# Gate logits of six token tiles summed on VectorE instead of multiplied on TensorE, and new distances between the operands in SBUF

## The chip, the cores and the metric

The kernel runs on one core of one Trainium2 chip. The metric is the device time of one execution in microseconds (us). A core has TensorE (PE, with its weight loads shown apart as PEld), VectorE (DVE), ScalarE (ACT), GpSimd (POOL) and SyncE (SP, which issues most DMAs). Each engine takes its instructions in the order written, and waits for the others through semaphores.

## The reference

Windowed attention makes 1152 token rows of 512 columns. A first mixture of four experts with given weights follows, then a second mixture of eight experts, where a gate sends each token to one expert:

```python
x = attention(q, k, v)                        # (1152, 512), window of 64
for e in range(4):                            # first mixture: every token, every expert
    out += p[:, e:e+1] * (maximum(x @ w1[e], 0) @ w2[e])
x = out
logits = x @ w_gate + modality_bias[modality_id]     # w_gate is (512, 8)
e_idx = argmax(logits, axis=1)
gate_w = softmax(logits)[arange(N), e_idx]
for e in range(8):                            # second mixture: a token's own expert alone
    h = maximum(x[e_idx == e] @ m2w1[e], 0)
    out[e_idx == e] = gate_w * (h @ m2w2[e])
```

The change touches `x @ w_gate`, for tokens 0 to 767, and where the tensors of all layers lie.

## The kernel before

**Tiles and stages.** The 1152 tokens are nine tiles of 128. A product in full precision is three products of rounded parts: tokens x are held as `xh` + `xl`, hidden rows as `hh` + `hl`, weights as `wh` + `wl`. Expert 0 runs interleaved with the attention. Experts 1, 2 and 3 each run over three groups g of 384 tokens (`moe1_group`): a **first layer** of eight blocks f (`mm1_at`, 12 matmuls of 384 columns each, weights stationary, tokens moving, line L343), then a **second layer** of three token tiles j in four parts each (`mm2_part`, 6 matmuls of 512 columns per part, hidden rows stationary, weights moving, L368). The second mixture follows in slots of 256 or 352 tokens with the same two layers.

**What follows a block.** After block f ACT writes `hh` (L352), then DVE writes `hl` (L353); that frees the block's PSUM bank. There are three such banks in turn, shared by both layers: block f=3 uses the bank of f=0, the second layer's tile j=0 that of f=5. After tile j DVE adds the result to `acc` (L379). Part p of tile j=0 reads `hl` of blocks 2p and 2p+1.

**Hooks.** After each block or part a hook may issue other work; the order is written by hand. In expert 3 the gate's logits are made one group later than their tokens: in group 1 for tiles 0 to 2, in group 2 for tiles 3 to 5. `gate_T` turns a token tile with four PE transposes (L751) and splits it in three bf16 parts (two ACT, two DVE instructions: L754 to L757); `gate_L` does twelve bf16 matmuls of 24 columns (L767); `gate_V`, after f=4, makes softmax and choice on DVE in a chain of small instructions, each waiting for the one before. `select_P` (after f=6 of group 1, one small matmul `psC`, L813) and `phase1` (after f=6 of group 2, two matmuls `psR`, L828 and L829) follow it. Tiles 6 to 8 are gated later.

**Where tensors lie.** In bytes of a partition, modulo 512, the built program has: the identity `ident` 128; `xh`, `xl`, `hh`, `hl`, `acc` and all `wh`, `wl` 384. Their column slices and blocks are multiples of 512 bytes apart, but the token tiles of `acc` are 2080 bytes apart, as are the seven buffers `xr` of gathered tokens.

Of the kernel before, what the change touches and what calls it, by code (L numbers as in the profile page):

```python
# [5 lines left out]
F32 = mybir.dt.float32  # L6
# [3 lines left out]
ACTF = mybir.ActivationFunctionType  # L10
ALU = mybir.AluOpType
# [4 lines left out]
def build(tc, q, k, v, probs, w1, w2, mid, wg, mbias, m2w1, m2w2, out):  # L16
    nc = tc.nc
    B, H, S, D = q.shape
    E, DM, FF = w1.shape
    NT = B * S  # L20
    NTILE = NT // 128
    HP = H // 2
    KD = DM // 128
    KF = FF // 128
    G0, G1 = 128, 256
    GT = 384
    NG = NT // GT
    ctx = ExitStack()
    with ctx:
        const = ctx.enter_context(tc.tile_pool(name="const", bufs=1))  # L30
# [11 lines left out]
        ident = const.tile([128, 128], F32, name="ident")  # L42
        mk = const.tile([128, 3, 128], F32, name="mk")
        prob = const.tile([128, NTILE, E], F32, name="prob")
        psumw = const.tile([128, 24], F32, name="psumw")[:, 0:NTILE].rearrange("p (t o) -> p t o", o=1)
        xh = big.tile([128, HP, NT], F32R, name="xh")
        xl = big.tile([128, HP, NT], F32R, name="xl")
        hh = big.tile([128, KF, GT], F32R, name="hh")
        hl = big.tile([128, KF, GT], F32R, name="hl")
        acc = big.tile([128, NTILE, 520], F32, name="acc")  # L50

        ident4 = big.tile([128, 56], F32, name="ident4")[:, 0:32]

        with tc.manual_schedule():

# [335 lines left out]
            def moe1_group(e, c0, n, hook):  # L391

                for f in range(KF):
                    mm1_at(f, c0, n)
                    hook("1", f, 0)
                mm2_group(e, c0, n, hook)
# [58 lines left out]
            def L(fn, *a):  # L455
                return lambda: fn(*a)
# [191 lines left out]
            for i in range(4):  # L648
# [36 lines left out]
            OHC = m2.tile([128, NTILE + 1, E2], BF16, name="OHC")  # L685

            nc.sync.dma_start(out=wgf, in_=wg.rearrange("(c p) e -> p c e", p=128))
            nc.sync.dma_start(out=mb.rearrange("p m e -> p (m e)"),
                              in_=mbias.rearrange("m e -> (m e)").partition_broadcast(128))
            nc.sync.dma_start(out=midi, in_=mid.bitcast(I32).rearrange("(t p w) -> p t w", p=128, w=2))  # L690
# [38 lines left out]
            def vv(out, a, b, op):  # L729
                nc.vector.tensor_tensor(out=out, in0=a, in1=b, op=op)  # L730
# [7 lines left out]
            def red(out, a, op=ALU.add):  # L738
                nc.vector.tensor_reduce(out=out, in_=a, axis=AX.X, op=op)
# [20 lines left out]
            def gate_L(t):  # L760
# [4 lines left out]
                for c in range(KD):  # L765
                    for i in range(3):
                        nc.tensor.matmul(out=psL[g][:, j], lhsT=x[i][:, c, :], rhs=wgb[:, c],  # L767
                                         start=(c == 0 and i == 0), stop=(c == KD - 1 and i == 2))

            def gate_V(g):  # L770
                sl = slice(3 * g, 3 * g + 3)
                lg = m2.tile([128, 3, E2], F32, tag="lg", name="lg", bufs=2)
                ex = m2.tile([128, 3, E2], F32, tag="ex", name="ex", bufs=2)
                mx = m2.tile([128, 3, 1], F32, tag="mx", name="mx", bufs=2)
                red(lg, psL.pop(g).rearrange("p j i e -> p j e i"))
                vv(lg, lg, biasm[:, sl, :], ALU.add)
                red(mx, lg, ALU.max)
                vv(lg, lg, mx.to_broadcast([128, 3, E2]), ALU.subtract)
                nc.scalar.activation(out=ex, in_=lg, func=ACTF.Exp)

                vs(lg, lg, 0.0, ALU.is_ge)
                vv(lg, lg, rev.to_broadcast([128, 3, E2]), ALU.mult)
                red(mx, lg, ALU.max)
                vv(OH[:, sl, :], lg, mx.to_broadcast([128, 3, E2]), ALU.is_equal)
                nc.vector.tensor_copy(out=OHb[:, sl, :], in_=OH[:, sl, :])
                for t in range(3 * g, 3 * g + 3):
                    vv(OHC[:, t + 1, :], OHC[:, t, :], OHb[:, t, :], ALU.add)
                gt = acc[:, sl, DM:DM + 1]
                red(gt, ex)
                vs(gt, gt, 1e-9, ALU.add)  # L790
                nc.vector.reciprocal(out=gt, in_=gt)
                nc.sync.dma_start(out=x2d[GT * g:GT * (g + 1), :].rearrange("(t p) d -> p t d", p=128),
                                  in_=acc[:, sl, :])
# [252 lines left out]
            def std(g):  # L1046
                def hook(kind, idx, part):
                    if g == 0 and kind == "1" and idx % 2 == 1:
                        split_next()
                    if g == NG - 1 and kind == "2" and idx < 2 and part in (0, 2):  # L1050
                        split_next()
                return hook
# [15 lines left out]

            for e in range(1, E - 1):
                for g in range(NG):  # L1070
                    moe1_group(e, GT * g, GT, std(g))

            def gating(g0):
                t = {}
                for f in range(3):
                    t.setdefault(("1", f, 0), []).append(L(gate_T, 3 * g0 + f))
                    t.setdefault(("1", f + 2, 0), []).append(L(gate_L, 3 * g0 + f))
                t["1", 4, 0].append(L(gate_V, g0))
                return t

            t1 = gating(0)
            t1["1", 6, 0] = [select_P, pump]
            t2 = gating(1)
            t2["1", 6, 0] = [phase1]
            t2["2", 0, 2] = [L(ids_mm, 1, 6)] + [L(gather, 1, a, 2 * GT) for a in range(A1)]
            t2["2", 1, 0] = [between]
# [2 lines left out]
            t2["2", 1, 1] = [L(gate_T, 6)]  # L1089
            t2["2", 2, 0].append(L(gate_L, 6))  # L1090
            t2["2", 2, 2] = [L(gate_T, 7)]
            moe1_group(E - 1, 0, GT, std(0))
            moe1_group(E - 1, GT, GT, at_hook(t1, std(1)))
            moe1_group(E - 1, 2 * GT, GT, at_hook(t2, std(2)))

# [185 lines left out]
```

## Time and profile before

| | |
|---|---|
| three runs | 595.76, 595.93, 595.97 us, median 595.93 |
| the profiled execution | 595.89 us, of which its span in the trace 594.1 us |
| outside the span | 1.79 us |
| PE busy | 585.4 us (99%) |
| DVE busy | 248.6 us (42%) |
| ACT busy | 192.1 us (32%) |
| POOL busy | 83.4 us (14%) |

Matmuls overlap in the pipeline and their ends are modelled, so 99% does not say that PE is at its peak; the distance from one matmul's start to the next one's tells more. Start times of the timeline are us from the span's start.

### The profile page before, as it was taken

The page shows a single profiled execution, that of the slowest core. Times are in us where ns is not written, and L with a number is a line of the kernel's source. Part 1 is how long each engine was busy: PE and PEld are TensorE (multiplying, and loading weights), DVE is VectorE, ACT ScalarE, POOL GpSimd, SP SyncE. Part 2 cuts the span into 40 slices and gives each one's busy share as a digit, 9 for nine tenths or more (in the row PEclk, how much of TensorE's full clock was granted, in tenths as well). Part 3 has the DMA queues.
Part 4 walks back from the last instruction along what each step waited for, and adds up shares of the span by engine and source line. Part 5 has one row for each costly group of instructions (what it writes and reads, how often), then busy time and mean ns, then how long its engine had stood idle before and what let it go on. Part 6 is the DMA issues. An engine that isn't in the chain of part 4 may idle for free. (4 is left out here: it accounts for less than half of the span.)

```text
span 594.1 us, 9420 instructions
## 1 busy us (share of the span) xinstructions
PE 585.4 (99%) x3818; PEld 517.0 (87%) x3818; DVE 248.6 (42%) x534; ACT 192.1 (32%) x373; POOL 83.4 (14%) x129
## 2 busy tenths in 40 slices
PE   8999999999999999999999999999999999999996
PEld 7798797979898989899898989899898989897964
DVE  4954545363462212524121243335168597233410
ACT  5853434352340101313020222222043455233421
POOL 3851212022000000000000000000002105323221
PEclk9999999999999999999999999999999999999999
DMA  8996460000521000224000040002306277316530
GB/s 212 201 254 99 89 196 1 2 2 1 143 76 68 0 1 0 75 67 135 9 0 1 1 142 1 0 1 69 127 2 203 79 269 210 133 54 207 189 90 31
DMA packets 55919, 51.11 MB, mean 86 GB/s; under 512 B 41151, under 2 KB 41151, under 8 KB 55872
## 3 DMA queue, kind: packets, MB, share of 16 engines
q1 hardware_dynamic: 53664, 45.05, 27.7%
q0 software_dynamic: 1680, 5.29, 2.6%
q8 instruction: 31, 0.51, 0.4%
q10 hardware_dynamic: 528, 0.13, 0.1%
q14 instruction: 16, 0.13, 0.1%
HBM read 45.71 MB, written 4.95 MB: 85 GB/s over the span
## 5 line engine op out<-in xcount | busy, mean ns | idle before, releaser
L343 PE MATMUL ps<-xh,wh 128*128 128x384 f32 (+2 forms) x544 | 173.5, 319 | 0.0
L343 PE MATMUL ps<-xh,wl 128*128 128x384 f32 (+2 forms) x544 | 171.7, 316 | 0.0
L343 PE MATMUL ps<-xl,wh 128*128 128x384 f32 (+2 forms) x544 | 171.5, 315 | 0.0
L368 PE MATMUL ps<-wh,hh 128*128 128x512 f32 (+1 forms) x368 | 147.2, 400 | 0.3 <-DVE hl L353 0.3
L368 PE MATMUL ps<-wh,hl 128*128 128x512 f32 (+1 forms) x368 | 144.0, 391 | 0.0
L368 PE MATMUL ps<-wl,hh 128*128 128x512 f32 (+1 forms) x368 | 143.8, 391 | 0.0
L352 ACT ACTIVATE hh<-ps 128x384 fp32r<-128x384 f32 (+2 forms) x112 | 52.0, 464 | 260.4 <-PE ps L343 255.8
L353 DVE SCALAR_TENSOR_TENSOR hl<-ps,hh 128x384 fp32r<-128x384 f32 (+2 forms) x112 | 58.2, 522 | 118.6 <-ACT hh L352 118.6
L343 PEld LDWEIGHTS ps<-xh,wh 128*128 128x128 f32 x544 | 103.0, 189 | 0.9 <-issue 0.3
L343 PEld LDWEIGHTS ps<-xl,wh 128*128 128x128 f32 x544 | 103.0, 189 | 0.5
L343 PEld LDWEIGHTS ps<-xh,wl 128*128 128x128 f32 x544 | 102.9, 189 | 0.0
L368 PEld LDWEIGHTS ps<-wh,hh 128*128 128x128 f32 (+1 forms) x368 | 68.8, 187 | 16.7 <-issue 2.2
L368 PEld LDWEIGHTS ps<-wh,hl 128*128 128x128 f32 (+1 forms) x368 | 68.7, 187 | 15.3
L368 PEld LDWEIGHTS ps<-wl,hh 128*128 128x128 f32 (+1 forms) x368 | 68.8, 187 | 13.3
L379 DVE SCALAR_TENSOR_TENSOR acc<-ps,prob,acc 128x512 f32<-128x512 f32 x27 | 20.3, 750 | 94.9 <-PE ps L368 94.9
L1019 POOL DMA_INDIRECT xr<-x2d,idg x11 | 12.5, 1137 | 317.5 <-DVE ids L730 314.9
L171 DVE TENSOR_TENSOR wl<-raw,wh 128x1024 fp32r<-128x1024 f32 x42 | 52.0, 1253 | 8.8 <-ACT wh L167 8.8
L167 ACT ACTIVATE wh<-raw 128x1024 fp32r<-128x1024 f32 x48 | 49.1, 1052 | 0.0
L277 ACT ACTIVATE sm<-sm,st 128x128 f32<-128x128 f32 x72 | 23.2, 391 | 5.4 <-DVE st L266 5.4
L294 POOL TENSOR_TENSOR sm<-sm,rs 128x512 f32<-128x512 f32 (+1 forms) x20 | 19.5, 976 | 26.3 <-DVE rs L287 24.3
L257 DVE SCALAR_TENSOR_TENSOR sm<-psS,mk 128x256 f32<-128x256 f32 (+1 forms) x40 | 14.0, 391 | 19.0 <-PE psS L245 17.7
L1042 POOL DMA_INDIRECT out_dram<-y,ids x11 | 11.3, 1024 | 58.5 <-ACT y L1040 37.2
(189 smaller groups left out, 413.1 us busy)
## 6 DMA issues: line engine op xcount, KB each, us to landing
raw<-in_moe_w_dram SPq DMA_DIRECT2D x60, 512.0 KB, 4.0
x2d<-acc SPq DMA_DIRECT2D x3, 780.0 KB, 3.8
va<-in_v_dram SPq DMA_DIRECT2D x8, 256.0 KB, 5.1
vb<-in_v_dram SPq DMA_DIRECT2D x16, 128.0 KB, 4.5
acc<-in_moe_w_dram SPq DMA_DIRECT2D x4, 512.0 KB, 8.6
acc<-in_q_dram SPq DMA_DIRECT2D x6, 128.0 KB, 4.3
qu<-in_q_dram SPq DMA_DIRECT2D x3, 256.0 KB, 4.0
ku<-in_k_dram SPq DMA_DIRECT2D x3, 256.0 KB, 4.8
```

The source lines that it names most:

```text
L167: nc.scalar.activation(out=hi, in_=x, func=ACTF.Copy)
L171: eng.tensor_tensor(out=lo[:, o], in0=x[:, o], in1=hi[:, o].bitcast(F32), op=ALU.subtract)
L257: nc.vector.scalar_tensor_tensor(out=p[:, h], in0=ps[:, h, 0:128 * nj].rearrange("p (j c) -> p j c", j=nj), scalar=0.125, in1=m, op0=ALU.m ...
L277: nc.scalar.activation(out=p[:, h, j], in_=p[:, h, j], func=ACTF.Exp, bias=st[:, o:o + 1])
L294: nc.gpsimd.tensor_tensor(out=p, in0=p, in1=rs.rearrange("p (h j) o -> p h j o", h=2).to_broadcast([128, 2, nj, 128]), op=ALU.mult)
L343: nc.tensor.matmul(out=ps[:, 0:n], lhsT=a[kk][:, fs], rhs=b_[:, kk, gs], start=(kk == 0 and term == 0) if first is None else (first and te ...
L352: nc.scalar.activation(out=hi, in_=ps[:, 0:n], func=ACTF.Relu)
L353: nc.vector.scalar_tensor_tensor(out=lo, in0=ps[:, 0:n], scalar=0.0, in1=hi.bitcast(F32), op0=ALU.max, op1=ALU.subtract)
L368: nc.tensor.matmul(out=ps[0:m], lhsT=a[:, f, ts_], rhs=b_[c][:, o:o + 512], start=(f == 0 and i == 0), stop=(f == KF - 1 and i == 2))
L379: nc.vector.scalar_tensor_tensor(out=o, in0=ps, scalar=prob[:, t, e:e + 1], in1=o, op0=ALU.mult, op1=ALU.add)
L1019: nc.gpsimd.indirect_dma_start(out=x, out_offset=None, in_=x2d[0:last, :], in_offset=bass.IndirectOffsetOnAxis(ap=idg[i][:, a:a + 1], axis=0))
L1042: nc.gpsimd.indirect_dma_start(out=out, out_offset=bass.IndirectOffsetOnAxis(ap=ap, axis=0), in_=y[0:m], in_offset=None, bounds_check=NT - ...
```

## The change

Six tiles no longer pass through `gate_T` and `gate_L`. `gate_D(t, e_)` takes one tile and one of the eight experts: a DVE instruction multiplies the tile's 512 columns by that expert's gate weights and sums them along the row into one logit per token. 48 of them are issued, two per hook, 24 for each three tiles: 16 during tiles j=1 and j=2 of one group's second layer, 8 after blocks f=0 to 3 of the next group. All 48 write the same scratch tile `gjunk`. For this the gate's weights must stand in each partition: once, after f=4 of group 1 of expert 1, `turn_wg` turns them with one PE transpose, stores them to DRAM with four DMAs and loads eight rows with eight DMAs that repeat a row in all 128 partitions. The eight rows lie in buffers that later hold gathered tokens and outputs.

Pads and one tensor's place change too. Modulo 512 the built program now has `xh`, `xl` at 480, `hh`, `hl`, `acc`, `wh`, `wl` at 256, `ident` still at 128. So tokens and weights of the first layer, which stood at distance 0, stand at distance 224; hidden rows and weights of the second layer stay at distance 0.

```diff
-        psumw = const.tile([128, 24], F32, name="psumw")[:, 0:NTILE].rearrange("p (t o) -> p t o", o=1)
+        psumw = const.tile([128, 48], F32, name="psumw")[:, 0:NTILE].rearrange("p (t o) -> p t o", o=1)
         xh = big.tile([128, HP, NT], F32R, name="xh")
         xl = big.tile([128, HP, NT], F32R, name="xl")
+        ident4 = big.tile([128, 72], F32, name="ident4")[:, 0:32]
         hh = big.tile([128, KF, GT], F32R, name="hh")
         hl = big.tile([128, KF, GT], F32R, name="hl")
-        acc = big.tile([128, NTILE, 520], F32, name="acc")
-        ident4 = big.tile([128, 56], F32, name="ident4")[:, 0:32]
+        acc = big.tile([128, NTILE * 520 + 56], F32, name="acc")[:, 0:NTILE * 520].rearrange("p (t d) -> p t d", d=520)
...
+            def turn_wg():
+                ps = pa.tile([KD * E2, 128], F32, tag="T", name="psWG")
+                nc.tensor.transpose(out=ps, in_=wgr.rearrange("p c e -> p (c e)"), identity=ident)
+                nc.scalar.activation(out=wgt, in_=ps, func=ACTF.Copy)
+                for c in range(KD):
+                    nc.sync.dma_start(out=wgd[:, 128 * c:128 * (c + 1)], in_=wgt[E2 * c:E2 * (c + 1), :])
+                for e_ in range(E2):
+                    nc.sync.dma_start(out=wge[e_][:, 0:DM], in_=wgd[e_, :].partition_broadcast(128))
...
+            def gate_D(t, e_):
+                nc.vector.scalar_tensor_tensor(out=gjunk, in0=acc[:, t, 0:DM], scalar=1.0, in1=wge[e_][:, 0:DM],
+                                               op0=ALU.mult, op1=ALU.mult, accum_out=lgd[:, t, e_:e_ + 1])
...
             def gate_V(g):
...
-                red(lg, psL.pop(g).rearrange("p j i e -> p j e i"))
-                vv(lg, lg, biasm[:, sl, :], ALU.add)
+                if g < 2:
+                    vv(lg, lgd[:, sl, :], biasm[:, sl, :], ALU.add)
+                else:
+                    red(lg, psL.pop(g).rearrange("p j i e -> p j e i"))
+                    vv(lg, lg, biasm[:, sl, :], ALU.add)
...
             def gating(g0):
-                t = {}
-                for f in range(3):
-                    t.setdefault(("1", f, 0), []).append(L(gate_T, 3 * g0 + f))
-                    t.setdefault(("1", f + 2, 0), []).append(L(gate_L, 3 * g0 + f))
-                t["1", 4, 0].append(L(gate_V, g0))
-                return t
+                before, t = {}, {}
+                for n in range(8):
+                    before["2", 1 + n // 4, n % 4] = [L(gate_D, 3 * g0 + n // 4, 2 * (n % 4) + i) for i in range(2)]
+                for n in range(4):
+                    t["1", n, 0] = [L(gate_D, 3 * g0 + 2, 2 * n + i) for i in range(2)]
+                t["1", 4, 0] = [L(gate_V, g0)]
+                return before, t
```

On DVE, before the change, the end of expert 3's group 0 and the first blocks of group 1 stand so (`ps` and a number is a PSUM bank of a block or tile):

```order
L379 SCALAR_TENSOR_TENSOR acc<-ps_3572,prob,acc 128x512
L379 SCALAR_TENSOR_TENSOR acc<-ps_3598,prob,acc 128x512
L379 SCALAR_TENSOR_TENSOR acc<-ps_3624,prob,acc 128x512
L353 SCALAR_TENSOR_TENSOR hl<-ps_3650,hh 128x384
L755 TENSOR_TENSOR xg<-psGT,xg_3670 128x512
L757 TENSOR_TENSOR xg_3672<-xg,xg_3671 128x512
L353 SCALAR_TENSOR_TENSOR hl<-ps_3678,hh 128x384
L755 TENSOR_TENSOR xg<-psGT,xg_3698 128x512
L757 TENSOR_TENSOR xg_3700<-xg,xg_3699 128x512
```

And with the change (L791 is `gate_D`; x6 is six in a row):

```order
L379 SCALAR_TENSOR_TENSOR acc<-ps_3601,prob,acc 128x512
L791 SCALAR_TENSOR_TENSOR gjunk,lgd<-acc,wge 128x512 x6
L379 SCALAR_TENSOR_TENSOR acc<-ps_3627,prob,acc 128x512
L791 SCALAR_TENSOR_TENSOR gjunk,lgd<-acc,wge 128x512 x8
L379 SCALAR_TENSOR_TENSOR acc<-ps_3661,prob,acc 128x512
L791 SCALAR_TENSOR_TENSOR gjunk,lgd<-acc,wge 128x512 x2
L353 SCALAR_TENSOR_TENSOR hl<-ps_3695,hh 128x384
L791 SCALAR_TENSOR_TENSOR gjunk,lgd<-acc,wge 128x512 x2
L353 SCALAR_TENSOR_TENSOR hl<-ps_3712,hh 128x384
L791 SCALAR_TENSOR_TENSOR gjunk,lgd<-acc,wge 128x512 x2
```

The second layer, where DVE had one instruction per tile, now holds sixteen `gate_D`, and two stand between any two `hl` of the next first layer's first blocks, in the place of L755 and L757.

On PE, before the change, the seam between blocks f=1 and f=2 of expert 3's group 1 reads (`psGT` is the bank of the turned tile):

```order
L343 MATMUL ps_3678<-xl,wh_3397 128x384
L343 MATMUL ps_3678<-xh,wl_3398 128x384
L751 MATMUL psGT<-ident,acc 128x128 x4
L343 MATMUL ps_3706<-xh,wh_3341 128x384
L343 MATMUL ps_3706<-xl,wh_3341 128x384
```

With the change the first interruption that PE meets in that first layer is `psC`, after f=6:

```order
L343 MATMUL ps_3812<-xl,wh_3426 128x384
L343 MATMUL ps_3812<-xh,wl_3427 128x384
L840 LDWEIGHTS ones
L840 MATMUL psC<-OHC,ones 128x8
L343 MATMUL ps_3868<-xh,wh_3370 128x384
L343 MATMUL ps_3868<-xl,wh_3370 128x384
```

All `psGT` and `psGL` of tiles 0 to 5 are gone from PE; those of tiles 6 to 8 stay where they were.

On SP the twelve DMAs of `turn_wg` stand between weight loads, as these rows of the changed program show:

```order
L704 DMA wgd<-wgt 8x128 x4
L706 DMA wge<-wgd 128x512 x8
```

## Rows read from the trace of the kernel before

**Rows 1.** The page: span, and PE's busy time, share and instructions.

```profile
span 594.1 us, 9420 instructions
PE 585.4 (99%) x3818; PEld 517.0 (87%) x3818; DVE 248.6 (42%) x534; ACT 192.1 (32%) x373; POOL 83.4 (14%) x129
...
PEclk9999999999999999999999999999999999999999
```

**Rows 2.** Groups by line and form, PE: count, busy us, mean ns, idle before.

```profile
L343 PE MATMUL ps<-xh,wh 128*128 128x384 f32 x288 | 97.5, 339 | 0.0
...
L343 PE MATMUL ps<-xh,wh 128*128 128x256 f32 x192 | 55.3, 288 | 0.0
...
L343 PE MATMUL ps<-xh,wh 128*128 128x352 f32 x64 | 20.8, 325 | 0.0
```

**Rows 3.** Timeline of PE, expert 3, group 0: start us, duration us, instruction.

```profile
359.14 0.33 PE L343 MATMUL ps<-xh,wh 128*128 128x384 f32 x1
...
375.81 0.39 PE L368 MATMUL ps<-wh,hh 128*128 128x512 f32 x1
...
392.17 0.33 PE L343 MATMUL ps<-xh,wh 128*128 128x384 f32 x1
```

**Rows 4.** Timeline of PE, group 1's first layer, with gating of tiles 0 to 2.

```profile
409.33 0.18 PE L813 MATMUL psC<-OHC,ones 128*128 128x8 bf16 x1
...
411.56 0.39 PE L368 MATMUL ps<-wh,hh 128*128 128x512 f32 x1
```

**Rows 5.** Timeline of PE, group 2's first layer, with gating of tiles 3 to 5.

```profile
427.92 0.33 PE L343 MATMUL ps<-xh,wh 128*128 128x384 f32 x1
...
445.09 0.20 PE L828 MATMUL psR<-OHb,tri 128*128 128x56 bf16 x1
...
447.33 0.39 PE L368 MATMUL ps<-wh,hh 128*128 128x512 f32 x1
```

**Rows 6.** Groups by line and form, DVE: count, busy us, mean ns, idle before.

```profile
L353 DVE SCALAR_TENSOR_TENSOR hl<-ps,hh 128x384 fp32r<-128x384 f32 x72 | 39.9, 555 | 78.6 <-ACT hh L352 78.6
L379 DVE SCALAR_TENSOR_TENSOR acc<-ps,prob,acc 128x512 f32<-128x512 f32 x27 | 20.3, 750 | 94.9 <-PE ps L368 94.9
...
L181 DVE TENSOR_TENSOR wl<-raw,wh 128x512 fp32r<-128x512 f32 x8 | 6.8, 862 | 1.3 <-ACT wh L177 1.3
...
L257 DVE SCALAR_TENSOR_TENSOR sm<-psS,mk 128x128 f32<-128x128 f32 x8 | 1.9, 284 | 8.5 <-PE psS L245 8.3
```

**Rows 7.** Timeline of DVE, end of group 0; in brackets idle time before, and its releaser.

```profile
392.37 0.75 DVE L379 SCALAR_TENSOR_TENSOR acc<-ps,prob,acc 128x512 f32<-128x512 f32 x1 [4.69 <-PE ps L368]
```

**Rows 8.** Timeline of DVE, group 1: `hl` of f=4, `gate_V`'s start, `hl` of f=5, f=6.

```profile
405.47 0.56 DVE L353 SCALAR_TENSOR_TENSOR hl<-ps,hh 128x384 fp32r<-128x384 f32 x1 [1.89 <-ACT hh L352]
405.95 0.22 DVE L739 TENSOR_REDUCE lg<-psGL 128x24 f32<-128x72 f32 x1
406.21 0.18 DVE L730 TENSOR_TENSOR lg<-lg,biasm 128x24 f32<-128x24 f32 x1
...
409.37 0.53 DVE L353 SCALAR_TENSOR_TENSOR hl<-ps,hh 128x384 fp32r<-128x384 f32 x1
410.05 0.56 DVE L353 SCALAR_TENSOR_TENSOR hl<-ps,hh 128x384 fp32r<-128x384 f32 x1 [0.16 <-ACT hh L352]
```

**Rows 9.** Timeline of DVE, group 2: `hl` of f=7, behind `phase1`.

```profile
450.29 0.55 DVE L353 SCALAR_TENSOR_TENSOR hl<-ps,hh 128x384 fp32r<-128x384 f32 x1
```

**Rows 10.** Groups by line and form, PE: transposes of the nine token tiles.

```profile
L751 PE MATMUL psGT<-ident,acc 128*128 128x128 f32 x36 | 5.5, 275 | 0.0
```

**Rows 11.** Timeline of PE: first layer behind an interruption (138), and undisturbed (142 to 145).

```profile
138.69 0.28 PE L343 MATMUL ps<-xl,wh 128*128 128x256 f32 x1
...
139.04 0.28 PE L343 MATMUL ps<-xl,wh 128*128 128x256 f32 x1
...
142.63 0.28 PE L343 MATMUL ps<-xl,wh 128*128 128x256 f32 x1
...
145.51 0.28 PE L343 MATMUL ps<-xl,wh 128*128 128x256 f32 x1
```

More of the change, by code (lines that the diff above doesn't have):

```diff
@@ L687, in build @@
             nc.sync.dma_start(out=wgf, in_=wg.rearrange("(c p) e -> p c e", p=128))
+            wgd = dram.tile([E2, DM], F32, name="wgd")
+            wgr = m2.tile([128, KD, E2], F32, name="wgr")
+            wgt = m2.tile([KD * E2, 128], F32, name="wgt")
+            wge = [m2.tile([128, XR], F32, tag="xr", name="wge", bufs=7) for _ in range(7)]
+            wge.append(m2.tile([128, DM], F32, tag="y", name="wge", bufs=3))
+            gjunk = m2.tile([128, DM], F32, tag="y", name="gjunk", bufs=3)
+            lgd = m2.tile([128, 6, E2], F32, name="lgd")
+            nc.sync.dma_start(out=wgr, in_=wg.rearrange("(c p) e -> p c e", p=128))
+            def turn_wg():
[6 more added lines that the diff above has]
+                    nc.sync.dma_start(out=wge[e_][:, 0:DM], in_=wgd[e_, :].partition_broadcast(128))
             nc.sync.dma_start(out=mb.rearrange("p m e -> p (m e)"),
@@ L1070, in build @@
                 for g in range(NG):
-                    moe1_group(e, GT * g, GT, std(g))
+                    moe1_group(e, GT * g, GT, at_hook({("1", 4, 0): [turn_wg]} if e == 1 and g == 1 else {}, std(g)))
             def gating(g0):
-                t = {}
-                for f in range(3):
-                    t.setdefault(("1", f, 0), []).append(L(gate_T, 3 * g0 + f))
-                    t.setdefault(("1", f + 2, 0), []).append(L(gate_L, 3 * g0 + f))
-                t["1", 4, 0].append(L(gate_V, g0))
-                return t
-            t1 = gating(0)
+                before, t = {}, {}
[5 more added lines that the diff above has]
+                return before, t
+            t0, t1 = gating(0)
             t1["1", 6, 0] = [select_P, pump]
-            t2 = gating(1)
+            t1b, t2 = gating(1)
+            t1.update(t1b)
             t2["1", 6, 0] = [phase1]
@@ L1091, in build @@
             t2["2", 2, 2] = [L(gate_T, 7)]
-            moe1_group(E - 1, 0, GT, std(0))
+            moe1_group(E - 1, 0, GT, at_hook(t0, std(0)))
             moe1_group(E - 1, GT, GT, at_hook(t1, std(1)))
```

## The prediction

> **What bounds the kernel now.** I read the page first: PE is busy for 99% of the span, and its granted clock is full (2.4 GHz) in all forty slices [rows 1]. A busy share of PE says little by itself, so next I read the timeline of PE, from one start to the next. In group 0 of expert 3, which holds no gating, the first layer runs from 359.14 to 375.81, 96 matmuls in 16.67 us, 173.6 ns each; at 2.4 GHz 384 columns stream in 160 ns, so 13.6 ns come on top. The second layer takes 72 matmuls to 392.17, 16.36 us, 227.2 ns each, again 13.9 ns over its 213.3 [rows 3]. There are no gaps: matmul stands behind matmul. DVE meanwhile sits idle 4.69 us before it can add a tile, waiting for PE [rows 7]. So here PE's own work sets the end, and what PE no longer does comes off the time as long as nobody makes it wait.
>
> The price of gating on PE is seen by setting a first layer with it beside one without. Group 1 needs 392.17 to 411.56, that is 19.39 us [rows 3, 4]; group 2 needs 427.92 to 447.33, 19.41 us [rows 5]. The regular layer needs 16.67. The excess holds the transposes, the small matmuls and the slower restart of the first layer behind each.
>
> **The terms.** (1) *Removed from PE.* Not all of the excess goes: `psC` and `psR` stay. The last block with `psC` lasts 409.33 to 411.56, 2.23 us, where a block has 16.67/8 = 2.08, so `psC` costs 0.15 [rows 3, 4]; with `psR` 447.33 − 445.09 = 2.24, so 0.16 [rows 5]. Removed are 19.39 − 16.67 − 0.15 = 2.57 and 19.41 − 16.67 − 0.16 = 2.58, together **5.15 us**.
>
> (2) *Added to PE.* `turn_wg` puts one transpose between two blocks, a single small instruction as `psC` is: **0.15 us**. Its copy on ACT is one small instruction. Its twelve DMAs go to SP some 11 us into a first layer that starts 165 us before the one of rows 3 (five groups of 16.67 + 16.36), so at about 205; the first `gate_D` comes behind the first tile of the second layer at 375.81 + 5.45 = 381. Behind the waiting DMAs on SP stand only the weight loads that the end of the next group asks for, over 30 us later. I cost them at nothing; the cover is more than 100 us.
>
> (3) *Added to DVE.* 48 `gate_D`, each a multiply-and-sum over 512 columns with both inputs in SBUF. No such instruction is in the trace. The same form of operation takes 284 ns for 128 columns and 555 for 384, 135 ns per 128, so 690 for 512; the adder L379, with a scalar read from memory, takes 750; the slowest row of 512 columns, L181, takes 862 [rows 6]. I take 0.72, between the two nearest, because an extra output is written, and keep 0.69 and 0.86 as ends. As all write `gjunk`, each waits for the one before; behind an instruction of 0.22 us the next of such a chain starts after 0.26, so 0.04 comes on top, while one that need not wait starts 0.08 before the end of the one ahead (405.95, behind 405.47 + 0.56) [rows 8].
>
> Is it hidden? For one group of three tiles: from the hook behind part 0 of tile j=1 to where `hl` of f=4 can start, PE needs 2 × 5.45 − 1.36 + 5 × 2.08 = 19.94 us, and `hl` starts 0.72 after its block's end (409.33 to 410.05 [rows 4, 8]): 20.66. In it DVE has 24 `gate_D`, two adds (2 × 0.67) and four `hl` (4 × 0.475), both less the early start, 0.04 for each of some 14 chained steps in the second layer, and 0.04 less for each of four pairs that stand between two `hl` and 0.08 less for each add behind a chain: 24 d + 1.34 + 1.90 + 0.56 − 0.16 − 0.16 = 24 d + 3.5. At d = 0.69 that is 20.1, at 0.72 20.8, at 0.75 21.5: DVE keeps up, or is up to 0.8 late. Who waits for late `hl`? `gate_V` follows as before and shifts with it. In group 1 `hl` of f=5 ends at 409.90 and the second layer, which takes that bank, starts at 411.56: 1.66 us of slack [rows 4, 8]. In group 2 `hl` of f=7 ends at 450.84; part 3 of tile j=0 reads it after 18 matmuls, at 447.33 + 4.1 = 451.4, so 0.6 of slack [rows 5, 9]. So up to about d = 0.74 the cost is **0**; beyond, each 0.01 costs 0.24 us in group 2, and from 0.79 on 0.24 in group 1 too. At the end 0.86, DVE is 3.5 late and PE waits 3.5 − 0.6 and 3.5 − 1.7, together 4.7 us.
>
> (4) *Addresses.* All matmuls of all first layers, 3 × (288 + 192 + 64) = 1632 [rows 2], read tokens at a new distance from the weights loaded meanwhile. The trace of before has only distance 0 for these operands, so nothing shows the new one. Ends: the whole overhead of 13.6 ns goes, 1632 × 13.6 = 22 us less; or it grows by as much, 22 us more. What is nearest: PE transposes read the nine token tiles of `acc`, 2080 bytes apart and so at nine places modulo 512, against one `ident`; the 36 have a mean of 275 ns [rows 10]. They have 128 columns only, so a stall could hide there behind the weight load, but it is the only row with different distances. I take **0**.
>
> Sum: 594.1 − 5.15 + 0.15 = 589.1 for the span, and 1.79 outside it: **590.9 us**. The profiled execution's own 595.89 is 0.04 from the median of the runs, so the same holds against that. About 0.2% (1.2 us) is what a measurement of this kernel can tell from no change.
>
> **The rivals.** *A. The distances help.* For: the overhead is no fixed constant of the stream. Behind an interruption three first-layer matmuls of 256 columns start 0.35 us apart in all, 117 ns each; undisturbed, 24 of them take 2.88 us, 120 ns each [rows 11]. Same operands, same distance, another phase between the two reads, and 3 ns less: they meet somewhere. Against: nothing says that 224 is a better place than 0. At 3 ns each, 1632 × 3 = 4.9 us: 586.0; with half the overhead gone 11 us, 580. Faster blocks also leave DVE 5 × 0.1 less slack, some tenths of a us.
>
> *B. The distances hurt.* The same reasoning the other way: 3 ns more each give 595.8, no change.
>
> *C. `gate_D` runs at half rate, and the kernel is slower.* If multiplying two SBUF inputs and summing takes two cycles a column, 512 columns cost 512 × 135/128 = 540 ns more, d = 1.23. DVE then needs 33.0 us for 20.66, is 12.4 late, and PE waits 12.4 − 0.6 and 12.4 − 1.7 in its two groups: 22.5 us, 613. From about d = 0.87 on PE's gain of 5.0 is eaten. Against it: plain two-input instructions of 512 columns in SBUF are at most 862 ns [rows 6], so two reads alone don't halve the rate; but none of those sums. The Trainium skill (Vector Engine (DVE) Microarchitecture Reference, Points that are easy to get wrong) states this very rule: the two-input scalar form loses half its throughput with two SBUF sources that are not bf16, for want of a port to read the accumulator. By that rule this rival is what happens; no row of before tests it.
>
> *D. PE's saving is given back later.* A wait that PE's work now hides could take its place: from group 2 on the hidden loads for the second mixture follow DVE's choice of experts, which keeps its distance to PE from f=4 on, as before. I see none; were half the gain lost, 593.5; all, 596.
>
> **Chances.** The forecast (gain counted, DVE hidden, addresses nothing, within 1 us) 0.44; A 0.28, of which a quarter below 582; B 0.07; C 0.10, and milder DVE stalls of some us (d from 0.78 to 0.95) 0.05, half of them still faster; D 0.06, half of it still faster. Faster by over 0.2%: 0.44 + 0.28 + 0.025 + 0.03, and a little of B: 0.78. Same: most of B, a part of D and of the stalls: 0.09. Slower: C and some of B: 0.13. The range leaves out C and the far part of A, and reaches to B: **582 to 596.5**. The likeliest case's own range is 589.9 to 592.
>
> **What would show it.** Right: regular first layers of 16.67 us as before, no `psGT` or `psGL` among the blocks of expert 3, and its groups 1 and 2 with first layers of 16.8; `gate_D` at 0.69 to 0.75 us, and `hl` of f=7 done before part 3. Wrong: first layers of experts 1 and 2, far from any gating, shorter or longer than 16.67 (A or B: each us over the kernel is 0.6 ns a matmul); `gate_D` of 1.2 us, with PE idle before block f=2 or before tile j=0 and DVE named as releaser (C); everything in expert 3 shorter but a gap in a slot of the second mixture that was not there (D).

## The result, and the profile after

| | before | after |
|---|---|---|
| median of four runs beside each other | 595.95 us (595.76 to 596.42) | 589.40 us (588.80 to 589.92) |
| profiled execution, and its span | 595.89, 594.1 | 589.92, 588.1 |
| ratio, 95% interval | | 0.9889 [0.9875, 0.9903] |

The kernel is 6.55 us faster, against the 5.0 forecast; the time lies 1.5 us below the forecast of 590.9.

The page of the changed kernel, span and busy times, answers to [rows 1]:

```profile
span 588.1 us, 9325 instructions
PE 579.4 (99%) x3723; PEld 512.2 (87%) x3723; DVE 272.3 (46%) x616; ACT 185.1 (31%) x362; POOL 83.3 (14%) x129
```

PE has 95 matmuls and 6.0 us of busy time less, DVE 23.7 us more. The span falls by as much as PE's busy time does, as it should if PE still sets the end.

The timeline of PE in expert 3 (start us, duration us, instruction), at the places of [rows 3 to 5]: group 0's first layer, its second layer, then the two first layers that had held the gating.

```profile
358.77 0.34 PE L343 MATMUL ps<-xh,wh 128*128 128x384 f32 x1
...
375.42 0.39 PE L368 MATMUL ps<-wh,hh 128*128 128x512 f32 x1
...
391.74 0.34 PE L343 MATMUL ps<-xh,wh 128*128 128x384 f32 x1
...
406.31 0.18 PE L840 MATMUL psC<-OHC,ones 128*128 128x8 bf16 x1
...
408.53 0.39 PE L368 MATMUL ps<-wh,hh 128*128 128x512 f32 x1
...
424.85 0.34 PE L343 MATMUL ps<-xh,wh 128*128 128x384 f32 x1
...
439.42 0.20 PE L855 MATMUL psR<-OHb,tri 128*128 128x56 bf16 x1
...
441.66 0.39 PE L368 MATMUL ps<-wh,hh 128*128 128x512 f32 x1
```

Read them as distances. Group 0: 375.42 − 358.77 = 16.65 us where before had 16.67, and 16.32 for the second layer where it had 16.36. Groups 1 and 2: 408.53 − 391.74 = 16.79 and 441.66 − 424.85 = 16.81, where before had 19.39 and 19.41. Two things have changed: 2.6 us left each gated first layer, as they should; and layers without any gating are 0.02 to 0.04 us shorter, which the forecast didn't have.

DVE's groups by line and form (count, busy us, mean ns, idle before), beside [rows 6]:

```profile
L353 DVE SCALAR_TENSOR_TENSOR hl<-ps,hh 128x384 fp32r<-128x384 f32 x72 | 39.9, 556 | 71.8 <-ACT hh L352 71.5
L791 DVE SCALAR_TENSOR_TENSOR gjunk<-acc,wge 128x512 f32<-128x512 f32 x48 | 33.1, 690 | 1.2
...
L791 DVE DVE_READ_ACCUMULATOR gjunk<-acc,wge 128x1 f32 x48 | 4.0, 82 | 0.0
```

`gate_D` takes 690 ns, and each is followed by a second instruction of 82 ns that fetches the sum. How the two pack shows in DVE's timeline at the start of the first chain and in the first blocks of group 1, where [rows 7] had an idle DVE:

```profile
381.06 0.75 DVE L379 SCALAR_TENSOR_TENSOR acc<-ps,prob,acc 128x512 f32<-128x512 f32 x1 [2.74 <-PE ps L368]
381.85 0.69 DVE L791 SCALAR_TENSOR_TENSOR gjunk<-acc,wge 128x512 f32<-128x512 f32 x1
382.46 0.08 DVE L791 DVE_READ_ACCUMULATOR gjunk<-acc,wge 128x1 f32 x1
382.58 0.69 DVE L791 SCALAR_TENSOR_TENSOR gjunk<-acc,wge 128x512 f32<-128x512 f32 x1
...
396.73 0.55 DVE L353 SCALAR_TENSOR_TENSOR hl<-ps,hh 128x384 fp32r<-128x384 f32 x1
...
400.79 0.56 DVE L353 SCALAR_TENSOR_TENSOR hl<-ps,hh 128x384 fp32r<-128x384 f32 x1 [0.18 <-ACT hh L352]
...
402.87 0.56 DVE L353 SCALAR_TENSOR_TENSOR hl<-ps,hh 128x384 fp32r<-128x384 f32 x1 [0.18 <-ACT hh L352]
```

One `gate_D` starts 0.73 us behind the last (381.85, 382.58). The `hl` of f=1 (396.73) follows without idle time: DVE is behind. At f=3 and f=4 it waits 0.18 us for ACT's `hh`: it has caught up, before `gate_V` starts. In group 2 `hl` of f=7, behind `phase1`, is [rows 9]'s row:

```profile
444.68 0.55 DVE L353 SCALAR_TENSOR_TENSOR hl<-ps,hh 128x384 fp32r<-128x384 f32 x1
```

It ends at 445.23; part 3 of tile j=0 starts 18 matmuls after 441.66, at 441.66 + 18 × 0.227 = 445.74. The slack of 0.5 us is a little less than the 0.6 of before, and nobody waits.

### The profile page after: what moved, and what is told of

The parts are those of the page before. It is cut to its first block, busy times and chain, and to the rows that moved or that the text cites. A ratio compares the mean times of both kernels' runs of the same rounds, so it can differ in the third digit from the quotient of the medians.

```text
span 588.1 us, 9325 instructions
## 1 busy us (share of the span) xinstructions
PE 579.4 (99%) x3723; PEld 512.2 (87%) x3723; DVE 272.3 (46%) x616; ACT 185.1 (31%) x362; POOL 83.3 (14%) x129
## 5 line engine op out<-in xcount | busy, mean ns | idle before, releaser
L368 PEld LDWEIGHTS ps<-wl,hh 128*128 128x128 f32 (+1 forms) x368 | 68.8, 187 | 13.2
L379 DVE SCALAR_TENSOR_TENSOR acc<-ps,prob,acc 128x512 f32<-128x512 f32 x27 | 20.3, 750 | 76.3 <-PE ps L368 76.3
L791 DVE SCALAR_TENSOR_TENSOR gjunk<-acc,wge 128x512 f32<-128x512 f32 x48 | 33.1, 690 | 1.2
```

The lines of the kernel that those rows point to most:

```text
L368: nc.tensor.matmul(out=ps[0:m], lhsT=a[:, f, ts_], rhs=b_[c][:, o:o + 512], start=(f == 0 and i == 0), stop=(f == KF - 1 and i == 2))
L379: nc.vector.scalar_tensor_tensor(out=o, in0=ps, scalar=prob[:, t, e:e + 1], in1=o, op0=ALU.mult, op1=ALU.add)
L791: nc.vector.scalar_tensor_tensor(out=gjunk, in0=acc[:, t, 0:DM], scalar=1.0, in1=wge[e_][:, 0:DM], op0=ALU.mult, op1=ALU.mult, accum_out=l ...
```

## The experiments

The theory to test: 5 us come from the matmuls that PE no longer does, DVE's new work is hidden with little to spare, and the rest of the gain comes from the new distances. Its rival: the distances do nothing, and the gated layers hide a gain or a cost that I missed. The kernel before ran beside each on the same chip (medians of 595.7 to 596.1). Starts of stages are compared between profiles from one mark on, the start of expert 0's first second layer. That mark lies between 47.6 and 49.0 us from the span's start, which hides effects of a microsecond; the landing of the first input loads may be the reason, but that is not shown. The medians include it too: two kernels below, *gate_only* and *dist256*, have the same distances modulo 256 and medians of 591.59 and 590.51 us, but from the mark on 540.86 and 540.78. The mark in before, after, gate_only and addr_only (the last two are described next):

```profile
48.38 0.40 PE L368 MATMUL ps<-wh,hh 128*128 128x512 f32 x1
...
48.80 0.40 PE L368 MATMUL ps<-wh,hh 128*128 128x512 f32 x1
...
48.97 0.40 PE L368 MATMUL ps<-wh,hh 128*128 128x512 f32 x1
...
47.95 0.40 PE L368 MATMUL ps<-wh,hh 128*128 128x512 f32 x1
```

With spans of 594.11, 588.13, 589.83 and 592.20 us, before needs 545.73 us from the mark to the span's end and after 539.33: 6.40 less.

### The two halves

*gate_only* is the changed kernel with the old places, all operands at 384:

```diff
-        psumw = const.tile([128, 48], F32, name="psumw")[:, 0:NTILE].rearrange("p (t o) -> p t o", o=1)
+        psumw = const.tile([128, 24], F32, name="psumw")[:, 0:NTILE].rearrange("p (t o) -> p t o", o=1)
...
-        ident4 = big.tile([128, 72], F32, name="ident4")[:, 0:32]
...
-        acc = big.tile([128, NTILE * 520 + 56], F32, name="acc")[:, 0:NTILE * 520].rearrange("p (t d) -> p t d", d=520)
+        acc = big.tile([128, NTILE, 520], F32, name="acc")
+        ident4 = big.tile([128, 56], F32, name="ident4")[:, 0:32]
```

> The changed kernel with the old places: tokens, hidden rows, acc and weights all at 384 mod 512, so first-layer distance 0; the gate on DVE stays. The changed kernel gained 6.0 us of span where the sum had 5.0. Theory 1 (the on-record sum: gate alone gains 5.0, addresses nothing; the rest is spread of the runs): the same time as the changed kernel, 589.4, first layers of 384 columns 16.64 us in both. Theory 2 (addresses give the missing 1 us): 590.4 to 590.9, matmuls of 256 columns again 120 ns from start to start, first layers 16.67.

*addr_only* is the kernel before with these same lines the other way round: gating on PE, new places.

> The kernel before with only the new places (tokens 480, the rest 256 mod 512), gating on PE as before. Theory 1: 595.9, no change. Theory 2: 594.7 to 595.2, first-layer matmuls of 256 columns about 118 ns in the mean instead of 120, those of 384 columns within 0.5 ns of before.

Measured: gate_only 591.59 us (591.19 to 591.75), ratio 0.9928 [0.9915, 0.9942]; addr_only 594.04 (593.77 to 594.95), 0.9976 [0.9965, 0.9986]. From the mark on, gate_only needs 540.86 us, 4.87 less than before, where the terms said 5.00; addr_only needs 544.25, 1.48 less. 4.87 + 1.48 = 6.35 of the 6.40: the halves add up to within 0.05. Most of what gate_only lacks of 5.00 is in one place, the first layer of expert 1's group 0, 16.81 us there, where a weight load waits once for an `hl` of DVE. Its timeline in expert 3, from group 1's first layer to group 2's second:

```profile
393.02 0.33 PE L343 MATMUL ps<-xh,wh 128*128 128x384 f32 x1
...
409.84 0.39 PE L368 MATMUL ps<-wh,hh 128*128 128x512 f32 x1
...
426.20 0.33 PE L343 MATMUL ps<-xh,wh 128*128 128x384 f32 x1
...
443.02 0.39 PE L368 MATMUL ps<-wh,hh 128*128 128x512 f32 x1
```

The two first layers that had held the gating take 16.82 us, as after's take 16.8, beside regular ones of 16.67.

### How much DVE work is hidden

Both kernels are the changed one with more products on DVE, of `gate_D`'s form but without the sum (692 ns each). *extra_f* adds one behind each of the blocks f=0 to 3, four per gated group:

```diff
+            def gate_X(t, e_):
+                nc.vector.scalar_tensor_tensor(out=gjunk, in0=acc[:, t, 0:DM], scalar=1.0, in1=wge[e_][:, 0:DM],
+                                               op0=ALU.mult, op1=ALU.mult)
-                    t["1", n, 0] = [L(gate_D, 3 * g0 + 2, 2 * n + i) for i in range(2)]
+                    t["1", n, 0] = [L(gate_D, 3 * g0 + 2, 2 * n + i) for i in range(2)] + [L(gate_X, 3 * g0 + 2, n)]
```

> The changed kernel with one more product of 512 columns on VectorE, without the sum, written to the same scratch tile, behind the two sums after each of blocks f=0 to 3 of the two gated first layers (8 more in all; nothing reads them). Theory 1 (VectorE was nearly full between two groups, and TensorE waits once its lateness passes 1.7 us in group 1 and 0.6 us in group 2): four more of 0.69 us make VectorE some 2.5 us late at f=4, and TensorE waits before tile j=0 in both groups and before part 3 in group 2, 3 to 4 us in all, 593. Theory 2 (VectorE has room to spare there): 589.4. The product without the sum takes 0.69 us by the slope of the rows, which would leave the sum's own cost as the difference.

*extra_2* adds them to the hooks in the second layer instead, eight per group:

```diff
-                    before["2", 1 + n // 4, n % 4] = [L(gate_D, 3 * g0 + n // 4, 2 * (n % 4) + i) for i in range(2)]
+                    before["2", 1 + n // 4, n % 4] = [L(gate_D, 3 * g0 + n // 4, 2 * (n % 4) + i) for i in range(2)] + [L(gate_X, 3 * g0 + n // 4, n % 4)]
```

> The changed kernel with one more such product behind the two sums of each of the eight hooks in the second layer (tiles j=1 and j=2), 16 more in all. Theory 1: eight more in a group are 5.9 us of VectorE where nothing is free; TensorE waits in both groups, first before f=2, whose bank tile j=2 still holds, then on late hidden rows: 9 to 10 us in all, 599. Theory 2: less than 3 us.

Measured: extra_f 594.58 us (592.42 to 595.50), ratio 0.9970 [0.9954, 0.9987]; extra_2 598.58 (597.59 to 599.10), 1.0039 [1.0024, 1.0053]. Group 1's first layer grows from 16.79 to 19.86 and 21.42 us, group 2's from 16.81 to 18.58 and 21.12; in extra_f the second layer between them also grows, from 16.32 to 16.94. That is 5.5 and 8.9 us over expert 3. (The six executions of extra_f spread widely, and the profiled one, 595.05 us, is among the longer.) The waits of PE (us in total, times, longest) name the places; first extra_f:

```profile
PE psC L844 <- DVE acc L759: 1.9, 1, 1.9
...
PE psR L859 <- DVE OHb L816: 1.1, 1, 1.1
```

and then extra_2:

```profile
PE ps L343 <- DVE acc L379: 4.7, 2, 2.4
```

None of the three stands among the waits of the changed kernel, where the longest wait of PE for DVE is 0.4 us. But the waits are not all that the work cost. Two stretches of extra_2 (us, then the engines' busy time, then the granted clock of TensorE as a share of 2.4 GHz, then DMA), and PE's timeline there:

```profile
396.00:400.00 4.00, 1.64 (x9) 1.50 (x9) 3.86 (x11) 0.49 (x1) 0.00 (x0) 1.00 0.00 0
400.00:404.00 4.00, 4.00 (x15) 3.92 (x15) 3.93 (x10) 0.49 (x1) 0.00 (x0) 0.57 0.00 0
...
398.50 0.45 PE L343 MATMUL ps<-xh,wh 128*128 128x384 f32 x1 [2.36 <-DVE acc L379]
...
400.62 0.52 PE L343 MATMUL ps<-xl,wh 128*128 128x384 f32 x1
...
402.86 0.52 PE L343 MATMUL ps<-xh,wl 128*128 128x384 f32 x1
```

PE stands idle for 2.36 us before block f=2, whose bank tile j=2's adder L379 frees late. Then it works on, and from 400.0 its steps are 0.32 us (402.86 − 400.62 is seven of them) where undisturbed ones are 0.173: 384 columns at 1.2 GHz, for eleven matmuls, while the granted clock of the stretch is 0.57. So of group 1's 4.6 us the wait with its restart is 2.6 and the lower clock 1.6; the rest is a short wait at `psC`. Group 2 has the same 2.6 and 1.6. In extra_f ten such slow matmuls follow group 1's wait of 1.9 us at `psC`, 1.0 us of them in the first layer and the 0.6 in the second. Group 2's waits there, 1.1 and 0.4 us before `psR`, are followed by none.

How much room DVE had in group 1 shows in extra_f, from the first layer's start to `hl` of f=4 on DVE, and on PE around `psC`:

```profile
391.41 0.34 PE L343 MATMUL ps<-xh,wh 128*128 128x384 f32 x1
...
404.74 0.55 DVE L353 SCALAR_TENSOR_TENSOR hl<-ps,hh 128x384 fp32r<-128x384 f32 x1
...
405.80 0.34 PE L343 MATMUL ps<-xh,wl 128*128 128x384 f32 x1
...
408.08 0.17 PE L844 MATMUL psC<-OHC,ones 128*128 128x8 bf16 x1 [1.94 <-DVE acc L759]
```

`hl` of f=4 comes 13.33 us behind the layer's start, in the changed kernel 402.87 − 391.74 = 11.13: DVE is 2.2 us late. `psC` starts 2.28 us behind the matmul before it, in the changed kernel 0.18: PE is held for 2.1. So the `gate_D` are hidden, but from `hl` of f=4 on only 0.1 us was to spare in group 1. Earlier there is more room: eight products in the second layer, 8 × 0.73 = 5.8 us, held PE for 2.5 at the bank. What waits first in extra_f is not a bank but `psC` and `psR`, which stand in PE's order after f=6 and need `gate_V`'s result. Neither that nor the lower clock was in what I expected of this run, which came out short.

### Distances in the first layer

Four kernels are the changed one with other pads, so that tokens stand at another distance from the weights, while hidden rows and weights stay at 0 from each other. Two numbers change; for *dist128* (tokens at 384):

```diff
-        psumw = const.tile([128, 48], F32, name="psumw")[:, 0:NTILE].rearrange("p (t o) -> p t o", o=1)
+        psumw = const.tile([128, 24], F32, name="psumw")[:, 0:NTILE].rearrange("p (t o) -> p t o", o=1)
...
-        ident4 = big.tile([128, 72], F32, name="ident4")[:, 0:32]
+        ident4 = big.tile([128, 96], F32, name="ident4")[:, 0:32]
```

> The changed kernel with the tokens at distance 128 instead of 224 from the weights (384 against 256 mod 512), all else in place. If distance does nothing, 589.4 and matmul steps as in the changed kernel. If distance sets how the two reads meet, the steps of 256 and 384 columns move by some ns, and the time by 1.6 us for each ns of all 1632 first-layer matmuls; the sign is open.

*dist256* (56 and 64 columns; tokens at 0) and *dist384* (88 and 32; tokens at 128):

> The changed kernel with the tokens at distance 256 from the weights (0 against 256 mod 512). If distance does nothing, 589.4. If it acts, steps differ from both distance 0 (120 and 173.6 ns) and 224 (about 118 and 173.4 ns); the sign is open.

> The changed kernel with the tokens at distance 384 from the weights (128 against 256 mod 512). After 0 (step over the stream 13.2, 14.3 and 13.7 ns for 256, 352 and 384 columns), 128 (12.0, 11.8, 15.6), 224 (11.7, 13.4, 13.4) and 256 (as 0): if the pattern repeats every 256 bytes, 384 behaves as 128: 12.0, 11.8 and 15.6 ns, and a time of about 591.5. If it repeats every 512 alone, other steps.

*d192* (40 and 80; tokens at 448), run later, beside the kernels at 32 and 64 further down:

> The changed kernel with the tokens at distance 192 from the weights, 64 before a multiple of 256; second layer at 0 as in the changed kernel. Theory 1 (cost goes by signed distance modulo 256): first layers of 96 matmuls lie between those at 224 (16.64 us) and those at 128 (16.85), total 589 to 591.5. Rival (224 is no place of a smooth curve but one good or bad slot among sixteen or so): 16.9 us or more, or under 16.55, and then 27 first layers and the slots move the total by over 2 us either way.

Measured: dist128 591.53 us (591.08 to 591.90), 0.9927 [0.9912, 0.9942]; dist256 590.51 (590.19 to 590.63), 0.9913 [0.9898, 0.9928]; dist384 591.01 (590.79 to 591.57), 0.9918 [0.9902, 0.9935]; d192 590.76 (590.50 to 590.84), 0.9916 [0.9901, 0.9931]. The totals lie close together; the steps tell more. This table is worked out from the traces: the mean distance between the starts of two undisturbed first-layer matmuls, less columns/2.4 ns, and one first layer of 96 matmuls of 384 columns.

| distance | 256 columns, ns | 352 | 384 | first layer, us |
|---|---|---|---|---|
| 0 (gate_only) and 256 | 13.2, 13.2 | 14.3, 14.4 | 13.7, 13.7 | 16.67 |
| 224 (after) | 11.7 | 13.4 | 13.4 | 16.64 |
| 192 | 7.9 | 13.4 | 16.5 | 16.96 |
| 128 and 384 | 12.0, 12.0 | 11.8, 11.8 | 15.6, 15.6 | 16.85 |

The distance does count. It counts modulo 256, as far as two pairs show it: 0 reads as 256, and 128 as 384. And no distance is best for all widths: 192 gives matmuls of 256 columns 5.3 ns and takes 2.8 ns from those of 384. That is no smooth curve between 224 and 128, as I had expected of d192: its first layer came out as the rival had it, its total did not, since the two widths cancel in part. Two rows of d192's timeline, 24 matmuls of 256 columns apart, show 2.72 us where [rows 11] have 2.88, and two more its first layer in expert 3, 16.96 where [rows 3] have 16.67:

```profile
139.91 0.28 PE L343 MATMUL ps<-xh,wh 128*128 128x256 f32 x1
...
142.63 0.28 PE L343 MATMUL ps<-xh,wh 128*128 128x256 f32 x1
...
358.68 0.34 PE L343 MATMUL ps<-xh,wh 128*128 128x384 f32 x1
...
375.64 0.39 PE L368 MATMUL ps<-wh,hh 128*128 128x512 f32 x1
```

The means of the table hide that the step is not fixed by the distance alone. In d192 `turn_wg`'s transpose interrupts one first layer, that of expert 1's group 1, after 60 matmuls. PE's timeline before it and behind it, up to the second layer:

```profile
192.25 0.34 PE L343 MATMUL ps<-xh,wh 128*128 128x384 f32 x1
...
202.67 0.34 PE L343 MATMUL ps<-xh,wl 128*128 128x384 f32 x1
...
203.48 0.34 PE L343 MATMUL ps<-xh,wh 128*128 128x384 f32 x1
...
209.20 0.40 PE L368 MATMUL ps<-wh,hh 128*128 128x512 f32 x1
```

Before the interruption 59 steps take 10.42 us, 176.6 ns each; behind it 33 take 5.72, 173.3 ns each, with operands at the same distance. Matmuls of 256 columns at 192 have two paces as well, 113.3 and 117.8 ns, and change from one to the other at interruptions. And layers of 384 columns at 0 and at 224 both settle at 173.3 ns: they differ in their first six steps, which are up to 185 ns at 0, and nowhere else.

### Distances in the second layer

*second224* moves `ident4` behind `hl`, so that hidden rows stand at 480 as the tokens do, 224 from the weights:

```diff
-        ident4 = big.tile([128, 72], F32, name="ident4")[:, 0:32]
         hh = big.tile([128, KF, GT], F32R, name="hh")
         hl = big.tile([128, KF, GT], F32R, name="hl")
+        ident4 = big.tile([128, 72], F32, name="ident4")[:, 0:32]
```

> The changed kernel with the hidden rows at 480 mod 512 beside the tokens, so that the second layer too has its operands at distance 224 (weights still 256, acc still 256). If what distance does depends on which operand moves and how long the stream is, the 1104 matmuls of 512 columns, 227 ns apart now, change their step by some ns: 1.1 us for each ns, sign open. If only the first layer is sensitive, 589.4 and 227 ns.

*second032* and *second064* widen the pad instead (80 and 88 columns), hidden rows at 288 and 320:

> The changed kernel with the hidden rows (and acc) 32 bytes further on, at 288: in the second layer the moving weights then stand 32 bytes before the stationary hidden rows, modulo 256. That is the same signed distance as in the first layer of the changed kernel (moving tokens 224 behind the weights, so 32 before the next multiple of 256); the kernel with hidden rows at 480 had the opposite sign and lost 0.46 us per second layer. Theory 1 (the signed distance of the moving from the stationary operand, modulo 256, sets the cost in both layers): the second layer stays at 16.3 us per 72 matmuls or a little less, first layers at 16.64, total 588.8 to 589.9. Rival (only how far the two are from a multiple of 256 counts, not the sign): second layer 16.78, total 594.5 to 595.7. Second rival (any distance but 0 costs the second layer): the same time as the first rival, told apart by the kernel at 64.

> The changed kernel with the hidden rows (and acc) at 320: the moving weights 64 bytes before the stationary hidden rows. No row so far shows 64 in either layer. Theory 1 says only that it goes the same way as the first layer with tokens at distance 192 in the kernel beside it (both are 64 before a multiple of 256): second layer between 16.2 and 16.8 us. If any distance but 0 costs the second layer: 16.6 or more, total over 593.

Measured: second224 595.18 us (594.35 to 595.51), 0.9986 [0.9976, 0.9995]; second032 594.85 (594.32 to 595.46), 0.9984 [0.9975, 0.9993]; second064 595.06 (594.67 to 595.86), 0.9990 [0.9981, 0.9999]. All three have second layers of 16.78 to 16.80 us, 72 matmuls, where the changed kernel has 16.32, and unchanged first layers. The timeline of PE in second224, expert 3's group 0, from the second layer's start to its end:

```profile
378.86 0.39 PE L367 MATMUL ps<-wh,hh 128*128 128x512 f32 x1
...
395.64 0.34 PE L342 MATMUL ps<-xh,wh 128*128 128x384 f32 x1
```

16.78 us is 233 ns a matmul, 6.4 more than after's 226.7. So the sign of the distance, my theory for second032, fell: 32 to either side, and 64, cost the same. What the three leave open is whether it is the distance from the weights or the hidden rows' own place, for only the hidden rows (in the last two with `acc`) were moved; a kernel with both at 480 was not run.

### A better version

*best* leaves the tokens where the changed kernel has them and moves the first layer's weights, by expert: 32 bytes for expert 0 and the first two of the second mixture (256 columns, and the third slot's 352), 96 bytes for the last.

```diff
+            def w_tile(nm, key, c):
+                o = {0: 8, "P0": 8, "P1": 8, "X": 8, "Q0": 24}.get(key, 0) if c < 4 else 0
+                return wp.tile([128, 1088 if c < 4 else 1024], F32R, tag=f"{nm}{c}", name=f"{nm}{c}")[:, o:o + 1024]
...
-                hi = wp.tile([128, 1024], F32R, tag=f"wh{c}", name=f"wh{c}")
-                lo = wp.tile([128, 1024], F32R, tag=f"wl{c}", name=f"wl{c}")
+                hi, lo = w_tile("wh", key, c), w_tile("wl", key, c)
...
-                wh[c] = wp.tile([128, 1024], F32R, tag=f"wh{c}", name=f"wh{c}")
-                wl[c] = wp.tile([128, 1024], F32R, tag=f"wl{c}", name=f"wl{c}")
+                wh[c], wl[c] = w_tile("wh", 0, c), w_tile("wl", 0, c)
```

> The changed kernel with the first-layer weights of expert 0 and of the slots' first two experts written 32 bytes further on in their buffers, and those of the last slot 96 bytes, so that their tokens stand at distance 192 (matmuls of 256 columns, and the third slot's 352) and 128 (the last slot's 352), while experts 1 to 3 keep 224. Here the stationary operand is moved, where the kernels before moved the tokens. Theory (the distance modulo 256 between moving and stationary operand sets the stall, whichever of them is moved): the 576 matmuls of 256 columns go from 11.7 to 7.9 ns over their columns, 2.2 us, the last slot's 96 of 352 from 13.4 to 11.8, 0.16 us; total 586.5 to 587.6. Rival (the tokens' own place counts, not the distance): 256 columns stay at 11.7, total 589.0 to 590.0, and the kernel with tokens at 192 gained there for its place alone.

Measured: 587.53 us (587.20 to 587.79), ratio 0.9858 [0.9842, 0.9874], the fastest here. The timeline of PE in expert 0 (24 matmuls of 256 columns apart) and in expert 3 (a first layer of 384):

```profile
139.94 0.28 PE L345 MATMUL ps<-xh,wh 128*128 128x256 f32 x1
...
142.66 0.28 PE L345 MATMUL ps<-xh,wh 128*128 128x256 f32 x1
...
356.94 0.34 PE L345 MATMUL ps<-xh,wh 128*128 128x384 f32 x1
...
373.59 0.39 PE L370 MATMUL ps<-wh,hh 128*128 128x512 f32 x1
```

2.72 us as in d192, and 16.65 as in the changed kernel: each width has the better of the two. In the first layer it is the distance that counts, whichever operand is moved. The means over all matmuls are 8.7 ns for 256 columns and 12.5 for 352, so 576 × 3.0 + 192 × 0.9 = 1.9 us, which is what the medians show (589.40 − 587.53). It is a little less than the 2.4 I expected: in the first group of expert 0 the 256 columns have 9.7 ns instead of d192's 7.0, in the first slot 10.3 instead of 8.5. In both places PE runs at the slower of the two paces, 117.8 ns, for a longer part of the layer; what chooses the pace was not tried.

## Why the prediction was right, and where it was not

**What bounds the kernel: right.** PE's instructions set the end before and after; 6.0 us less busy time on PE gave 6.0 us less span, and 24 us more on DVE added nothing that shows.

**(1) Removed from PE, 5.15 us: right.** Reading the price as one gated first layer less one regular one held: gate_only lost 2.57 and 2.58 us in them (19.39 to 16.82, 19.41 to 16.83).

**(2) `turn_wg`, 0.15 us: right.** Its first layer in gate_only has 16.78 us for 16.67, 0.11 more. Its DMAs cost nothing that shows.

**(3) `gate_D` hidden on DVE: right in size, with the wrong waiter.** I took 0.72 between ends of 0.69 and 0.86; it is 0.69, and the chained step 0.73 as the sum of 0.69 and 0.04 had it. The reading of the sum, 82 ns, is an instruction that I had not counted, but it lies in the end of the product. With 0.69 the working gave 20.1 us in a window of 20.7, half a microsecond early; the rows show DVE caught up at f=3 with 0.18 idle.

The step that failed is who would wait if it were late. I had put the slack at 1.66 us in group 1, at the bank of `hl` f=5. extra_f shows `psC` waiting first: with DVE 2.2 us late PE is held for 2.1 there, so the slack is 0.1 us. I let `gate_V` "shift with it" and didn't follow its result to the small matmul that PE meets after f=6. And my price for late DVE (4.7 us at the end 0.86) held the waits alone: behind each of the three waits of 1.9 to 2.4 us the lower clock cost another 1.6. For the limit, an estimate from the rows (DVE's `hl` of f=2, 3 and 4 start some 0.7 us in all later than DVE could have begun them, 18 `gate_D` lie in that chain, and 0.1 us is left behind it) has the cost at 0 up to about d = 0.73. I had 0.74, for another place in group 2, and 0.79 in group 1; that the first number is so close is luck.

**Rival C, half rate, 613 us: refuted.** `gate_D` takes 0.69 us for its 512 columns, where two cycles a column would have been 1.23. The rule on which it rested (the Trainium skill, Vector Engine (DVE) Microarchitecture Reference, Points that are easy to get wrong: the two-input scalar form loses half its throughput with two SBUF sources that are not bf16) doesn't hold for this row: both sources are float32 in SBUF. The measurement decides.

**(4) Addresses, taken as 0: this is the term that was off.** They gave 1.5 us from the mark on; by the medians 1.8 alone (594.04 beside 595.81) and 2.2 on top of the gate (589.40 beside 591.59), which include what differs ahead of the mark. So the time fell 0.5 us below the likeliest case's range of 589.9 to 592. Stage by stage, addr_only beside before, 0.8 us of the 1.5 are in the first layers of 256 and 352 columns, 0.25 in the nine of 384, and 0.36 in the nine second layers behind those, which are 0.04 us shorter each, though their distance is 0 as before. The nearest row I had, the 36 transposes with a mean of 275 ns, says nothing for these matmuls: it has 128 columns, and the effect differs with the width. Rival A was right in direction, with 3 ns where 0.3 to 1.5 came; that two reads meet somewhere is not shown. I read its evidence, 117 against 120 ns [rows 11], off a matmul of 256 columns, the width with the most to gain at 224, and spread it over all 1632. It is two paces at one distance, as d192 shows them too, and says nothing of what another distance does.

**Rival D, the saving given back later: no.** From the first matmul of the second mixture (466.23 us before, 460.53 after) to the span's end, before needs 127.9 us, after 127.6.

## What to carry to other kernels

Price work on a saturated engine as the length of a stage with it less the length of the same stage without, not as a sum of durations. When it goes to an idle engine, add the duration times the count, compare it with the window up to the next consumer, and follow the result to every small instruction that the saturated engine meets in order; here that was `psC`, not a bank. A wait of the saturated engine can cost more than itself: here three of some 2 us were followed by 1.6 us each at the lower clock. And on a kernel in which one matmul stands behind the other, the distance between the two operands in SBUF is a size to try for each width by itself, on whole layers, since the pace can change at an interruption: it moved the mean step by up to 5 ns of 120 in one direction and 3 of 174 in the other.

## What the runs showed of the hardware

- The mean step of back-to-back matmuls depends on where the moving operand lies against the stationary one: 114.5 ns (192), 118.4 (224) and 119.9 (0) for 256 columns; 173.4 (224), 173.7 (0) and 176.5 (192) for 384. Distances 256 apart read the same.
- It depends on what went before as well. At 192 there are two paces, 113.3 and 117.8 ns for 256 columns, 176.6 and 173.3 for 384, and an interruption can change one into the other (d192). So the two slots of 256 columns have means of 8.5 and 11.1 ns over the columns' time there, where expert 0's groups have some 7.
- Hidden rows moved by 32, 64 or 224 bytes cost each second-layer matmul of 512 columns in experts 1 to 3 6.4 to 6.7 ns; whether by their distance from the weights stays open.
- Second layers read no tokens, yet are 16.36 us with tokens at 0 and 16.32 at 224, all else in its place (dist256 and after). Only their first nine steps differ, 225 to 236 ns at 0; then both run at 226.7. So a layer starts otherwise by what ran ahead of it: in d192 the one second layer behind `turn_wg`'s interruption takes 16.36 us too, the regular ones 16.32.
- In extra_2 and extra_f the granted clock fell to 1.2 GHz for ten or eleven matmuls, steps of 0.32 us for 384 columns, after PE had stood idle for 1.9 to 2.4 us and taken up work again. Behind idle times of 1.1 and 0.4 us it did not fall.
- A multiply with a sum on DVE is two instructions in the trace, 690 and 82 ns, which start 0.61 us apart; without the sum the product takes 692.
